# When VectorE takes up an attention pair's sums: a reordering in a fused attention and gated MLP kernel

## The chip, the core and the metric

The kernel runs on one core of a Trainium2 chip. The metric is the device time of one execution in microseconds (us). The core has five engines that matter here, each with its own queue of instructions, worked off in order: TensorE (PE in the profile, its weight loads PEld), VectorE (DVE), ScalarE (ACT), GpSimd (POOL) and SyncE (SP), which starts nearly all DMAs. [...]

## What is computed

The first block is a linear attention without a softmax, for 8 batches, 8 heads, 576 positions and a head width of 64:

```
kv  = einsum('bhsd,bhse->bhde', k, v)          # k^T v, one 64x64 matrix a head
out = einsum('bhsd,bhde->bhse', q, kv)
rms = sqrt(mean(out * out, axis=-1) + 1e-06)   # the mean over a head's 64 values
x   = out / rms * g_norm
```

The heads of a position are then laid side by side, so that x is 4608 tokens of 512 values. The second block is a gated MLP with 2048 hidden values:

```
h = x @ w_in
g = h * erf(softplus(h))
y = g @ w_out
```

q, k, v and g_norm are 32 bit floats. The weights arrive as 64 bit floats, and the kernel turns them into 32 bit ones on the chip.

## The kernel before

**Groups and units.** The tokens are worked in groups of 512. Groups are numbered by `T`; the first group is T = 0. A group's MLP runs over 16 hidden chunks of 128 values, called units (`f`, or `n` counted on through the groups: unit 21 is chunk 5 of group 1). The loop over `n` writes the instructions of group 0 (n = 0 to 15) and group 1 (n = 16 to 31); a second loop, over batches of four units, writes all later groups. While a group's MLP runs, the attention of the next group is done beside it, in four pairs of heads (`p` = 0 to 3). So the second group's pairs (T = 1) lie beside the units 0 to 15, and the third group's (T = 2) beside the units 16 to 31.

**One unit of group 0** on TensorE is a product with w_in into `h_ps` (L1219, 8 matmuls in the profile) and, five units late (`LAG`), a product with w_out into the four `o_ps` (L856, 8 matmuls). ScalarE copies `h_ps` out (L1232) and applies softplus (L1248); each fourth unit it applies erf for four units (L1172). VectorE multiplies h by the result (`gates`, L1100).

**The conversion of the weights** runs beside group 0, item by item in the order `w_order`: one item is one or two chunks of w_in or w_out. Each item has a load (`load_w`, L244 and L249, into one of four `w_raw` buffers), a split on ScalarE (`w_split`, L271, into one of two `w_m` buffers) and a join on VectorE (`w_join`: L281, L284, L287 and L292, four instructions; the last one writes the finished chunk, `w_in_sb` or `w_out_sb`). `weights()` does the split of the next item, the join of the current one and the load of a later one. It is called at a unit's start if the next item falls `due`, and again, in a `while`, before the unit's matmuls.

**One attention pair** is made of pieces that `attention(T, p)` returns and `pieces_of` hangs on units. Each unit has four places: `steps[f][3]` runs at the unit's start, just after the first call of `weights()`; `steps[f][0]` follows it, still ahead of the `while`; `steps[f][1]` runs after the unit's softplus; `steps[f][2]` runs at its end.

- `visit` (the piece `apply`): TensorE computes the results of the pair and k^T v of the *next* pair into one PSUM tile, `at_ps` (L474, L479, L484). ScalarE squares the result o into the tile `qT` (L492), copies o out (L502), copies the two 64-partition halves of k^T v into `kv_other`, each crossed over to the other half of the partitions (L368), and copies the last 64 positions into `x_last` (L507).
- `keep` and `sums` (the piece `after`): VectorE adds the crossed halves to k^T v in `at_ps` and writes `bd_kv` (L372), which the next pair's `visit` needs. It then transposes the squares (L527) and sums them by block (L415, `ms`); for every second pair a few short copies bring the sums together (L428, L429).
- `root` (the roots, on ScalarE), `norm` (on VectorE, with the transposition of the next pair's q, L347) and `split` follow in later units.

`visit` of T = 1, p = 0 is hung on unit 5 (`steps[5][3]`), and its `keep` and `sums` follow at the same place. All other pairs have `visit` at `steps[f+1][1]` and `keep` and `sums` at `steps[f+1][2]`, the end of the same unit.

**The last pair of the third group** (T = 2, p = 3, `both` in the code) is special: its `visit`, in unit n = 29, computes k^T v for *two* next pairs, so that ScalarE makes four crossed copies. Right after it the last units of group 1 (n = 28 to 31) and the *held* units are worked off: four gated units 24 to 27, whose products with w_out are kept back until the MLP of group 1 ends. ScalarE and VectorE cut each of them into three forms, `g_held` (`hold_upper`, L735, on ScalarE; `hold_lower`, L738 and L741, on VectorE), and TensorE multiplies them last (L1116, `held_sums`). A unit of group 1 has two PSUM tiles, `n_ps` and `m_ps` (L800); ScalarE copies n_ps out (L1234) and VectorE adds m_ps (L775) before the next unit may write them. When the held sums are done and the last gates of group 1 are through (L1100), the memory that they held is freed, SyncE loads the first parts of w_out for the loop over batches (L1046), and that loop starts.

The functions that the diff touches:

Of the kernel before, what the change touches and what calls it, by code (L numbers as in the profile page):

```python
# [70 lines left out]
def kernel(  # L71
# [10 lines left out]
    nc = tc.nc  # L82
    P = 128
# [4 lines left out]
    R = S - G  # L88
# [144 lines left out]
    x_last = const.tile([P, KC, G], FP32, name="x_last")  # L233
# [100 lines left out]
    def halves_of(t):  # L334
        return t.rearrange("p (a t) -> p a t", a=2)

    def kv_of(T, p):
        return bd_kv[:, (T * NP + p) % 2, :]
# [10 lines left out]
    def kv_products(T, p, diagonal, beside, first=0):  # L349


        ks, vs = (x.pop((T, p)) for x in (k_sb, v_sb))
        for c in range(CH):
            for i, rows in enumerate(rows_of):
                half = (i + c + first) % 2
                yield half == i, partial(
                    nc.tensor.matmul,
                    (diagonal if half == i else beside)[rows_of[half]],
                    lhsT=ks[rows, c],
                    rhs=vs[rows, c],  # L360
                    start=(c < 2),
                    stop=(c >= CH - 2),
                )

    def kv_beside(at, other, copy, cols=kv_cols):

        for i in range(2):
            copy(other[rows_of[i]], at[rows_of[1 - i], ::-1, cols])  # L368
# [22 lines left out]
    def other_tile(n):  # L391
        t = attp.tile([P, 2, 2, D], FP32, name="kv_other", tag="kv_other")
        return t[:, 0:n]

    def at_tile():
        return at_pool(1).tile([P, 2, G], FP32, name="at_ps", tag="at")
# [14 lines left out]
    def small_tile(name):  # L411
        return attp.tile([P, 2 * BLOCKS], FP32, name=name, tag=name)
# [41 lines left out]
    def attention(T, p):  # L454

        st = {}

        alone = p > 1
        then = divmod(T * NP + p + 1, NP)
        both = (T, p) == (FIRST, NP - 1)  # L460
        more_cols = slice(kv_cols.stop, kv_cols.stop + D)

        two = halves_of

        bd = kv_of(T, p)

        def visit():


            qT = ready.pop((T, p))  # L470
            at = st["at"] = at_tile()
            x = halves_of(qT[:, 0:G])
            for s in rows_of:
                nc.tensor.matmul(  # L474
                    at[s, 1, 2 * P : 2 * P + R], lhsT=bd[s, D : 2 * D], rhs=qT[s, G:S], start=True, stop=True
                )
            st["o"] = at[:, :, 0 : 2 * P]
            for _, product_ in kv_products(*then, at[:, 1, kv_cols], at[:, 0, kv_cols], first=1):
                product_()  # L479
            if both:  # L480
                for _, product_ in kv_products(then[0], 1, at[:, 1, more_cols], at[:, 0, more_cols]):
                    product_()
            for a, i in ((0, 0), (0, 1), (1, 0), (1, 1)):
                nc.tensor.matmul(  # L484
                    at[rows_of[i if a else 1 - i], a, 0 : 2 * P],
                    lhsT=bd[rows_of[i], a * D : (a + 1) * D],
                    rhs=x[rows_of[i], a],
                    start=True,
                    stop=True,
                )  # L490
            st["sq"] = qT[:, 0:G]
            nc.scalar.activation(two(st["sq"]), st["o"], AF.Square, scale=0.125)  # L492
            if T < FIRST:
                if T not in xT:
                    xT[T] = wide.tile([P, KC, G], FP32, name="xT", tag="ab"[T])
                x = xT[T][:, p, :]
            elif p % 2:
                x = x_new.tile([P, G], FP32, name="x", tag="x")
            else:
                x = attp.tile([P, G], FP32, name="x_even", tag="sq_lo")  # L500
            st["x"] = x
            nc.scalar.copy(two(x), st["o"])  # L502
            others = st["others"] = other_tile(2)
            kv_beside(at, others[:, 0], nc.scalar.copy)
            if both:
                kv_beside(at, others[:, 1], nc.scalar.copy, more_cols)
            nc.scalar.copy(x_last[:, p, T * R : T * R + R], at[:, 1, 2 * P : 2 * P + R])  # L507

        def keep():
            others = st.pop("others")  # L510
            kv_sum(*then, st["at"], others[:, 0])
            if both:
                kv_sum(then[0], 1, st["at"], others[:, 1], more_cols)

        def sums():


            if not alone:
                if p == 0:
                    shared["ms"] = small_tile("ms")  # L520
                total = shared["ms"]
            else:
                total = small_tile("ms")
            st["ms"] = total
            side = p if not alone else 0
            t = attp.tile([P, G], FP32, name="sq_t", tag="rms_r")
            nc.vector.transpose(out=t, in_=st["sq"])  # L527
            sum_blocks(total, side, t)
            shared[side] = st
            if not alone and p == 0:  # L530
                return
            n = side + 1
            other = small_tile("ms_other")
            meet(total, other, nc.vector.tensor_copy, n)
            st["n"] = n

        def root(table=True):
            if "n" not in st:
                return
            total, n = st["ms"], st["n"]  # L540
            st["r"], st["u"] = small_tile("rms"), small_tile("rms_u")
            exp_ln_table()
            roots(total, st["r"], st["u"], n)
            if table:
                softplus_table()

        def norm():
            if "n" not in st:
                return
            n = st["n"]  # L550
            refine(st["ms"], st["r"], st["u"], n)
            for i in range(n):
                other = shared[i]
                rb, x = other.pop("sq"), other["x"]
                spread_over(rb, st["u"], i)
                nc.vector.scalar_tensor_tensor(
                    out=x, in0=x, scalar=gm_col, in1=rb, op0=ALU.mult, op1=ALU.mult
                )

        def split():  # L560
            if T < FIRST or "n" not in st:
                return
            for q_ in range(p + 1 - st["n"], p + 1):
                upper(shared[q_ % 2 if not alone else 0]["x"], x_forms[T][0][:, q_])
            for q_ in range(p + 1 - st["n"], p + 1):
                lower(shared[q_ % 2 if not alone else 0].pop("x"), *(form[:, q_] for form in x_forms[T]))

        def loads():
            i = T * NP + p + 2
            if i == (FIRST + 1) * NP + 1:  # L570
                load_q(i)
                load_kv(i + 1)
                load_kv(i + 2)
                return
            load_pair(i, later=True)
            if i == (FIRST + 1) * NP:
                load_kv(i + 1)

        first_ = (partial(prepare, T, p),) if (T, p) == (1, 0) else ()
        then_ = partial(turn, *then)  # L580
        pieces = (first_, (visit, loads), (keep, sums))
        return (*(partial(chain, *group) for group in pieces), root, partial(chain, norm, then_), split)


    twice = {}
# [464 lines left out]
    def pieces_of(T):  # L1050


        steps = [([], [], [], []) for _ in range(FC)]
        for p in range(NP):
            products, apply, after, mean, norm, split = attention(T, p)
            f = (BATCH - 1) * (p + 1) if T < FIRST else BATCH * p

            first = T < FIRST and p == 0
            steps[f][1].append(products)
            steps[f + 2 if first else f + 1][3 if first else 1].append(apply)  # L1060
            steps[f + 2 if first else f + 1][3 if first else 2].append(after)
            with_erf = (f + 2) % BATCH == BATCH - 1
            if T == FIRST and p == NP - 1:
                ending.extend((partial(mean, table=False), norm, split))
                continue
            steps[f + 2][1].append(partial(mean, table=not with_erf))
            steps[f + 3][0].append(norm)
            steps[min(f + 4, FC - 1)][0].append(split)
        return steps
# [5 lines left out]
    others = [("out", f) for f in (*range(FC - BATCH, FC), *range(FC - BATCH))]  # L1075
# [98 lines left out]
    for n in range(FIRST * FC + 1):  # L1174
        T, f = divmod(n, FC)
        if T < FIRST:
            if f == 0:
                steps = pieces_of(T + 1)
# [162 lines left out]
    for m in range(first_batch, batches + 1):  # L1341
        T, b = divmod(m, NB)
# [127 lines left out]
```

## Time and profile before

| what | value |
|---|---|
| median of 3 runs | 890.06 us (888.09 to 891.25) |
| the profiled execution's own time | 889.88 us |
| its span in the profile | 888.1 us |
| busy: PE, DVE, ACT | 874.7 us (98%), 750.4 us (84%), 551.8 us (62%) |
| the loop over batches (256 to 880 us), PE busy | 624.00 of 624.00 us |

The span is the time from the first to the last instruction that the profiler saw. Times in the profile are read from the span's start. In a timeline row the first number is the start, the second the time from the start of the first to the end of the last instruction of the row, then engine, line, operation, the tile written and the tiles read, shapes and the count; in brackets stands the engine's idle time before it and what ended it. Busy times of several engines overlap; what counts is which engine's idle time or work stands on the path that ends last.

### The profile page before, as it was taken

What the parts mean: (1) busy time and instruction counts of PE and PEld (TensorE: products, weight loads), DVE (VectorE), ACT (ScalarE), POOL (GpSimd) and SP (SyncE); (2) the same over time, 40 slices, a digit from 0 to 9 for tenths busy, and PEclk for the clock granted to TensorE, in tenths of its full rate; (3) what the DMA queues carried; (4) which work ended last, traced back from release to release, by engine and by line L of the source; (5) the groups of instructions that cost most, each with busy time, mean ns of one, the idle gap of its engine ahead of it and who ended that gap; (6) DMA issues with size and microseconds to landing.
All of it is one profiled execution on the core that took longest, in us unless ns stands there. A gap on an engine that the chain in (4) does not pass through costs nothing.

```text
span 888.1 us, 13265 instructions
## 1 busy us (share of the span) xinstructions
PE 874.7 (98%) x4842; PEld 653.7 (74%) x4842; DVE 750.4 (84%) x1117; ACT 551.8 (62%) x813; POOL 4.7 (1%) x14
## 2 busy tenths in 40 slices
PE   8989999999999999999999999999999999999998
PEld 4434446656778888888888888888888888888887
DVE  5868997799889898989898989898979797966667
ACT  5947776777665656656574747474756575755552
POOL 2000000000000000000000000000000000000000
PEclk9999999999999999999999999999999999999999
DMA  9964627889799997999699978998797778778861
GB/s 290 296 226 146 198 75 268 305 303 357 252 339 386 342 370 239 381 350 361 209 369 359 349 265 312 375 329 305 272 351 278 290 288 347 291 284 321 323 256 48
DMA packets 136928, 259.88 MB, mean 293 GB/s; under 512 B 78816, under 2 KB 87264, under 8 KB 136864
## 3 DMA queue, kind: packets, MB, share of 16 engines
q1 hardware_dynamic: 136128, 258.09, 81.7%
q10 hardware_dynamic: 544, 0.82, 0.3%
q8 instruction: 38, 0.62, 0.3%
q14 instruction: 26, 0.21, 0.1%
q0 software_dynamic: 192, 0.13, 0.0%
HBM read 224.40 MB, written 34.60 MB: 292 GB/s over the span
## 4 chain that ended last, share of the span: by engine, by line
PE 81%; DVE 8%; ACT 5%; DMA 3%; issue 2%; SPq 1%; DVEq 0%; ACTq 0%
PE n_ps L800 48%; PE m_ps L800 24%; PE h_ps L1219 2%; PE o_ps L856 2%; DVE w_e L287 1%; DMA w_out_parts<-w_out 1%; PE diag_ps L623 1%; PE at_ps L628 1%; DVE w_e L284 1%; ACT s_sb L1172 1%; DVE w_e L281 1%; DVE h_sb L1100 1%; ACT L117 1%; PE warm_ps L1004 1%; DMA w_raw<-in_moe_w_out_dram 1%
## 5 line engine op out<-in xcount | busy, mean ns | idle before, releaser
L800 PE MATMUL n_ps<-w_out_parts,g_forms 128*128 128x512 f32 (+1 forms) x936 | 230.3, 388 | 1.1 <-DMA w_out_parts<-w_out 1.1
L800 PE MATMUL n_ps<-x_forms,w_in_parts 128*128 128x512 f32 x896 | 222.7, 391 | 0.0
L800 PEld LDWEIGHTS n_ps<-w_out_parts,g_forms 128*128 128x128 f32 x936 | 175.1, 188 | 37.5 <-DMA w_out_parts<-w_out 1.8
L800 PEld LDWEIGHTS n_ps<-x_forms,w_in_parts 128*128 128x128 f32 x896 | 167.5, 188 | 38.1 <-issue 3.8
L775 DVE TENSOR_TENSOR h<-m_ps,h 128x512 f32<-128x512 f32 x116 | 78.5, 686 | 65.2 <-PE m_ps L800 65.1
L1381 ACT ACTIVATE s<-h 128x512 f32<-128x512 f32 x112 | 69.3, 632 | 88.3 <-DVE h L775 88.3
L800 PE MATMUL m_ps<-w_out_parts,g_forms 128*128 128x512 f32 x464 | 124.0, 390 | 0.0
L1376 ACT ACTIVATE h<-n_ps 128x512 f32<-128x512 f32 x112 | 66.7, 596 | 85.6 <-PE n_ps L800 83.6
L800 PE MATMUL m_ps<-x_forms,w_in_parts 128*128 128x512 f32 x448 | 119.8, 390 | 0.0
L800 PEld LDWEIGHTS m_ps<-w_out_parts,g_forms 128*128 128x128 f32 x464 | 87.1, 188 | 18.1
L800 PEld LDWEIGHTS m_ps<-x_forms,w_in_parts 128*128 128x128 f32 x448 | 84.1, 188 | 17.4
L775 DVE TENSOR_TENSOR e<-m_ps,e 128x512 f32<-128x512 f32 x116 | 80.1, 692 | 14.2 <-PE m_ps L800 3.7
L856 PE MATMUL o_ps<-w_out_sb,h_sb 128*128 128x512 f32 x192 | 87.1, 596 | 0.1
L735 ACT ACTIVATE g_forms<-h 128x1024 fp32r<-128x1024 f32 x58 | 60.8, 1060 | 39.8 <-PE m_ps L800 21.6
L741 DVE SCALAR_TENSOR_TENSOR g_forms<-g_forms 128x1024 fp32r<-128x1024 f32 x58 | 71.1, 1225 | 2.0
L738 DVE TENSOR_TENSOR g_forms<-h,g_forms 128x1024 fp32r<-128x1024 f32 x58 | 70.6, 1217 | 0.5 <-ACT g_forms L735 0.4
L856 PEld LDWEIGHTS o_ps<-w_out_sb,h_sb 128*128 128x128 f32 x192 | 35.9, 190 | 42.4 <-issue 37.9
L1430 DVE TENSOR_TENSOR h<-h,s 128x1024 f32<-128x1024 f32 x56 | 65.9, 1218 | 0.0
L1219 PE MATMUL h_ps<-xT,w_in_sb 128*128 128x512 f32 x128 | 59.5, 611 | 3.9 <-DVE w_in_sb L292 3.9
L770 DVE SCALAR_TENSOR_TENSOR e<-n_ps,e 128x512 f32<-128x512 f32 (+1 forms) x89 | 59.8, 672 | 4.2 <-PE n_ps L800 4.2
L117 ACT ACT_TABLE_LOAD x41 | 52.6, 1283 | 0.7
L1219 PEld LDWEIGHTS h_ps<-xT,w_in_sb 128*128 128x128 f32 x128 | 24.5, 195 | 36.1 <-issue 33.2
(159 smaller groups left out, 944.3 us busy)
## 6 DMA issues: line engine op xcount, KB each, us to landing
w_out_parts<-w_out SPq DMA_DIRECT2D x116, 768.0 KB, 7.3
w_in_parts<-w_in SPq DMA_DIRECT2D x112, 768.0 KB, 7.0
w_in<-w_new SPq DMA_DIRECT2D x16, 768.0 KB, 4.8
k_sb<-in_k_dram SPq DMA_DIRECT2D x32, 288.0 KB, 5.9
v_sb<-in_v_dram SPq DMA_DIRECT2D x31, 288.0 KB, 5.6
w_raw<-in_moe_w_in_dram SPq DMA_DIRECT2D x16, 512.0 KB, 5.6
w_raw<-in_moe_w_out_dram SPq DMA_DIRECT2D x8, 1024.0 KB, 4.9
out_dram<-e SPq DMA_DIRECT2D x32, 256.0 KB, 4.0
```

Source lines behind the costliest of these rows:

```text
L117: nc.scalar.preload_act_table_set("softplus")
L735: nc.scalar.activation(high, x, AF.Copy, scale=1.0 + 2.0**-13)
L738: nc.vector.tensor_tensor(out=low, in0=x, in1=high.bitcast(FP32), op=ALU.subtract)
L741: nc.vector.scalar_tensor_tensor(out=both, in0=low.bitcast(FP32), scalar=SHIFT, in1=high.bitcast(FP32), op0=ALU.mult, op1=ALU.add,)
L770: nc.vector.scalar_tensor_tensor(out=out_, in0=ps, scalar=scale, in1=out_, op0=ALU.mult, op1=ALU.add)
L775: nc.vector.tensor_tensor(out=out_, in0=ps, in1=out_, op=ALU.add)
L800: nc.tensor.matmul(ps[:, cols], lhsT=weights(form, k), rhs=moving(form, k)[:, cols], start=(form == forms[0] and k == 0), stop=(form == fo ...
L856: nc.tensor.matmul(o_ps[j], lhsT=g[:, j * P : j * P + P], rhs=one(w_out_sb, f), start=(f == 0), stop=last,)
L1219: nc.tensor.matmul(plain[i], lhsT=blocks_of(one(w_in_sb, i % FC))[:, c], rhs=xT[T][:, c, :], start=(c == 0), stop=(c == KC - 1),)
L1376: nc.scalar.activation(h[:, i], n_ps, AF.Copy, scale=SHIFT - 1.0)
L1381: nc.scalar.activation(s[:, i], h[:, i], AF.Softplus)
L1430: nc.vector.tensor_tensor(out=part(h, half), in0=part(h, half), in1=part(s, half), op=ALU.mult)
```

## The change

The pieces `keep` and `sums` of each pair move from the end of a unit (or, for T = 1, p = 0, from the same place as `visit`) to the start of the following unit, `steps[f+2][3]` (for T = 1, p = 0: `steps[f+3][3]`, unit 6), that is, behind the first call of `weights()` of that unit. For the last pair of the third group, the four crossed copies of k^T v and the copy into `x_last` go from ScalarE to VectorE, just ahead of the additions in `keep`, and ScalarE's copy of o goes to `steps[f+2][1]`, a unit later.

The instructions themselves are otherwise the same. In the order of the instructions on each engine only this differs between the two programs:

- VectorE, T = 1, p = 0: three instructions (L372, L527, L415) move behind one w_in item's join, one gate and one w_out item's join. Before, they stood between the gate ahead of that and the first of the joins.
- VectorE, T = 2, p = 3: five copies are added ahead of the two additions (L372).
- ScalarE, T = 2, p = 3: these five copies are gone, and the copy of o (L502) stands behind the first two `g_held`, one copy of n_ps and one softplus.
- TensorE, GpSimd and SyncE: nothing. For the six other pairs nothing moves on any engine: between their old place and their new one no other instruction stands.

```diff
@@ attention(T, p): visit
             st["sq"] = qT[:, 0:G]
             nc.scalar.activation(two(st["sq"]), st["o"], AF.Square, scale=0.125)
+            if not both:
+                copy_out()
+                beside(nc.scalar.copy)
+
+        def copy_out():
             if T < FIRST:
...
             st["x"] = x
             nc.scalar.copy(two(x), st["o"])
+
+        def beside(copy):
             others = st["others"] = other_tile(2)
-            kv_beside(at, others[:, 0], nc.scalar.copy)
+            at = st["at"]
+            kv_beside(at, others[:, 0], copy)
             if both:
-                kv_beside(at, others[:, 1], nc.scalar.copy, more_cols)
-            nc.scalar.copy(x_last[:, p, T * R : T * R + R], at[:, 1, 2 * P : 2 * P + R])
+                kv_beside(at, others[:, 1], copy, more_cols)
+            copy(x_last[:, p, T * R : T * R + R], at[:, 1, 2 * P : 2 * P + R])
 
         def keep():
+            if both:
+                beside(nc.vector.tensor_copy)
             others = st.pop("others")
             kv_sum(*then, st["at"], others[:, 0])
...
         pieces = (first_, (visit, loads), (keep, sums))
-        return (*(partial(chain, *group) for group in pieces), root, partial(chain, norm, then_), split)
+        later = copy_out if both else chain
+        return (*(partial(chain, *group) for group in pieces), later, root, partial(chain, norm, then_), split)
@@ pieces_of(T)
-            products, apply, after, mean, norm, split = attention(T, p)
+            products, apply, after, later, mean, norm, split = attention(T, p)
...
             steps[f][1].append(products)
             steps[f + 2 if first else f + 1][3 if first else 1].append(apply)
-            steps[f + 2 if first else f + 1][3 if first else 2].append(after)
+            steps[f + 3 if first else f + 2][3].append(after)
+            steps[f + 2][1].append(later)
```

## The prediction, made before the changed kernel ran

> **What bounds the kernel now.** I first asked the windows of busy time by stage, then the waits, then the timeline around the two places that the change touches. From 256 us to 880 us TensorE has no gap, so nothing can be won there, and whatever is won before moves that whole block forward. Three rows of the windows (columns: stretch, its length, PE busy, PEld, DVE, ACT, POOL, granted clock, DMA share, GB/s):
>
> ```profile
> 53.00:58.00 5.00, 5.00 (x9) 2.06 (x8) 4.79 (x7) 0.70 (x1) 0.00 (x0) 0.66 1.01 342
> ...
> 223.00:228.00 5.00, 5.00 (x15) 3.97 (x16) 4.82 (x13) 2.15 (x4) 0.00 (x0) 0.66 1.05 385
> ...
> 256.00:880.00 624.00, 624.00 (x3454) 513.00 (x3453) 534.31 (x755) 374.33 (x522) 0.00 (x0) 1.00 0.86 312
> ```
>
> The granted clock is 0.66 in the first two: a third of the cycles is missing, which is half clock for 3.4 of 5 us. Both stretches follow a TensorE gap, and the change touches both. The first, in the waits from 20 to 135 us:
>
> ```profile
> DVE bd_kv L372 <- ACT x_last L507: 8.2, 2, 5.1
> ...
> PE h_ps L1219 <- DVE w_in_sb L292: 3.9, 2, 3.2
> ```
>
> and in the timeline:
>
> ```profile
> 43.25 0.69 DVE L1100 TENSOR_TENSOR h_sb<-h_sb,s_sb 128x512 f32<-128x512 f32 x1
> ...
> 46.78 0.21 ACT L507 COPY x_last<-at_ps 128x64 f32<-128x64 f32 x1
> ...
> 47.03 0.29 DVE L372 TENSOR_TENSOR bd_kv<-at_ps,kv_other 128x128 f32<-128x128 f32 x1 [3.10 <-ACT x_last L507]
> ...
> 48.58 0.68 DVE L281 TENSOR_SCALAR w_e<-w_raw 128x1024 f32<-128x1024 f32 x1
> ...
> 52.65 5.37 PE L1219 MATMUL h_ps<-xT,w_in_sb 128*128 128x512 f32 x8 [3.18 <-DVE w_in_sb L292]
> ...
> 68.02 0.29 DVE L372 TENSOR_TENSOR bd_kv<-at_ps,kv_other 128x128 f32<-128x128 f32 x1 [5.13 <-ACT x_last L507]
> ```
>
> VectorE stands 3.10 us before pair 0's sums because ScalarE copies late; the w_in join queued behind them (48.58) comes late for it, and TensorE stands 3.18 us for that join. Its next 8 matmuls take 5.37 us where others of L1219 take 3.60. The second place, around 221 us:
>
> ```profile
> 220.07 1.08 ACT L368 COPY kv_other<-at_ps 64x128 f32<-64x128 f32 x4
> ...
> 221.40 0.49 DVE L372 TENSOR_TENSOR bd_kv<-at_ps,kv_other 128x128 f32<-128x128 f32 x2 [1.77 <-ACT x_last L507]
> ...
> 222.31 0.59 ACT L1234 ACTIVATE h<-n_ps 128x512 f32<-128x512 f32 x1
> ...
> 222.95 0.50 PE L800 MATMUL n_ps<-x_high,w_new 128*128 128x512 f32 x1 [1.79 <-ACT h L1234]
> ```
>
> **Part A, the sums of pair 0 behind two joins.** Removed from the path: VectorE's wait. The gate at 43.25 ends at 43.94; the join, 3.92 us long in the trace (48.58 to 52.50), can start at 43.97 and end at 47.89. Its w_raw was loaded by an issue at 28.70, and the split of it is ScalarE's L271 at 42.97 to 44.13, ahead of everything that is late. (Were it the next L271, 46.89 to 48.04, the join would end at 49.3.) TensorE's w_out products start at 45.88, and 8 of them take 3.43 us to the start of what follows (57.86 to 61.29), so TensorE asks for the chunk at 49.31 and finds it. Gain: 52.65 - 49.31 = 3.34 us. With no gap I expect no clock loss: 57.86 - 52.65 = 5.21 becomes 3.43, another 1.78. Sum 5.12 us; bounds 3.3 (the slow clock stays) and 5.3.
>
> Does it reach the end? The moved block's reader is pair 1's visit on TensorE, then at 64.82 - 5.12 = 59.70. VectorE's order is now join to 47.89, gate 0.60, join 3.95, block 1.55 (47.03 to 48.58), so the block ends at 53.99 and the transposed q, queued behind it, at about 54.8. That cover is some 5 us; without it TensorE would stand for the excess. VectorE then does what took 5.91 us before (56.98 to 62.89) and is at pair 1's sums at 59.9, while ScalarE's x_last is ready at 67.98 - 5.12 = 62.87. So it waits there 3.0 instead of 5.13 us, and its two waits shrink from 8.2 to 3.0, that is, by the same 5.1. From here TensorE, VectorE and ScalarE have their old distances, 5.12 us earlier, and up to 121 us neither TensorE nor VectorE waits again. SyncE's order is unchanged: its load behind the first join waits for L287, and goes 4.7 us earlier (51.31 to 46.6). The k and v that pair 1's visit needs follow it; 52.33 to 64.82 is 12.5 us for a transfer that lands after 4.4 to 6.1, so 0.4 us less costs nothing.
>
> **Part B, the last pair of the third group.** ScalarE loses the copy of o (0.59 from start to start), four copies (1.09) and x_last (0.10 to 0.21): the two g_held and the copy of n_ps behind them come 1.78 us earlier, at 220.6 for the latter. It then waits only for TensorE's n_ps, which began at 218.06; TensorE can go on at 221.2. The copy of o now stands between a softplus and two g_held, 0.5 us on ScalarE, which I cost at nothing: the softplus ahead of it waits for VectorE and comes earlier by about that.
>
> VectorE gains work: four 64x128 copies from PSUM. Nearest row: L387 copies of 64x128, 246.82 to 247.85 for four, 0.26 each, and 0.25 for x_last (L644, twice the size, took 0.28): 1.3 us, bounds 1.2 and 1.5. They start at 219.62, when the second gate ends, without waiting for ScalarE's copies. So the additions start at 220.9 instead of 221.40: VectorE is 0.5 us earlier, not 1.8. Queued behind it are the add that frees m_ps (224.09, then 223.6 to 224.2) and the four g_held lowers. TensorE, 1.7 us earlier at 221.2, has done its n_ps at 223.1 and now stands for m_ps until 224.2, then for g_held: the second unit's are ready at 228.03 - 0.48 = 227.55. From there TensorE has 0.92 us of products to go to where it stood at 229.24, so it is there at 228.47, 0.77 us earlier, and the chain behind it (e at 234.43, the last gate at 241.2, the load of w_out issued at 241.86) is paced by that. B is 0.8 us.
>
> Bounds of B: 1.8 above (the additions cost VectorE nothing). Below zero too: the slow clock of 223 to 228 may come back, because TensorE still stands about 1.1, 1.0 and 0.4 us in small pieces. Half clock for 3.4 us on the held products, where VectorE no longer hides it, costs 1.7: B = -0.9. [...]
>
> **Sum.** 5.1 + 0.8 = 5.9 us from the profiled execution's own 889.88 gives 884.0; that execution stands 0.18 below the median 890.06, so on the median's scale 884.2. With the slow clock in B it is 885.9. I forecast 884.4. This kernel's runs spread from 888.09 to 891.25, so about 0.3% (2.7 us) is what a measurement can tell: faster means below 887.4, slower above 892.7.
>
> **Rivals.**
> - *Only the wait goes, not the clock* (chance 0.12): TensorE's slow stretch at 53 us comes anyway, or another late input at 49.3 takes half of the gap. Against it: each low clock in these rows follows a gap. A is 3.3 or less, B near zero or below: 886.6 to 888.
> - *Swallowed by transfers* (0.09): DMA is at 0.90 share from 171 to 222 us and PE waits 1.06 us for w_out_parts at 254.75. If these loads are paced by the memory and not by their issue, the loop starts when it did: 889 to 890. Against it: SyncE's longest waits are for compute, and the w_out load waited 8.7 us for the gate L1100 at 241, so it moves along.
> - *Slower* (0.07): the new small gaps keep TensorE at half clock from 223 us on. Each us at half clock costs 0.5; to undo 5.9 and lose another 2.7 it takes 17 us of it, about all of TensorE's work up to 240. The price would be 893. Against it: both slow stretches in the trace end after 3.4 us, though TensorE was dense in them.
> - *The change does little of what it says*: the sums of seven pairs are moved in the code, but the order of instructions changes for pair 0 of the second group alone. So A rests on one place; it is the place with the gap.
>
> **How the numbers follow.** Forecast 0.72 (883 to 886.5, both clock cases of B), rivals 0.12, 0.09 and 0.07; the fourth is no time of its own. Low end: A 5.3 and B 1.8 give 883.0, and 0.8 for the spread of a median: 882.2. High end: the first rival, 888.0. Faster: 0.72 and two thirds of the first rival, 0.80; same 0.13; slower 0.07.
>
> **What the profile after would show.** Right: no wait of TensorE for w_in_sb near 49 us, clock 1.00 from 43 to 68, VectorE's first wait for x_last gone and the second about 3.0 us; at the last pair TensorE's wait for the n_ps copy gone, a new one of about 1 us for VectorE's add of m_ps; the loop over batches 4 to 6 us earlier and as long as before. Wrong: a new TensorE wait for bd_kv or q at 59.7, clock under 1.00 past 228 us, or a wait for w_out_parts longer by what was won.

## The result, and the profile after

The changed kernel takes 884.03 us (median of 16 runs, 882.87 to 889.0), beside 888.95 us for the kernel before in the same set (median of 16, 887.21 to 891.25). The ratio is 0.9952, with a 95% interval of 0.9939 to 0.9965. The profiled execution took 885.19 us, its span 883.4 us. The change adds lines, so that places have new numbers: L800 is now L813, L775 is L788, L1219 is L1233, L1116 is L1130, L1100 is L1114, L507 is L517, L738 and L741 are L751 and L754, L1046 is L1059. L368 and L372 stay.

The windows of busy time, in the stretches shown before (columns as there: stretch, length, PE, PEld, DVE, ACT, POOL, granted clock, DMA share, GB/s); the loop over batches now begins earlier, so its row ends at 875:

```profile
43.00:53.00 10.00, 10.00 (x24) 4.37 (x23) 9.59 (x13) 7.42 (x13) 0.00 (x0) 1.00 0.82 271
53.00:58.00 5.00, 5.00 (x13) 2.28 (x12) 4.90 (x7) 2.27 (x3) 0.00 (x0) 1.00 0.88 250
223.00:228.00 5.00, 5.00 (x19) 4.05 (x18) 4.68 (x9) 3.94 (x6) 0.00 (x0) 0.78 0.95 244
256.00:875.00 619.00, 619.00 (x3433) 508.83 (x3432) 530.29 (x749) 370.48 (x518) 0.00 (x0) 1.00 0.86 312
```

From 43 to 53 us TensorE has no gap any more, and from 53 to 58 us the granted clock is 1.00 (0.66 before). At the second place, from 223 to 228 us, it is 0.78. The waits from 20 to 135 us:

```profile
DVE bd_kv L372 <- ACT x_last L517: 3.1, 1, 3.1
...
PE h_ps L1233 <- DVE w_in_sb L292: 0.7, 1, 0.7
```

VectorE's 8.2 us in two waits have become one of 3.1; TensorE's 3.9 us have become 0.7, and that one is the other wait, at 23 us. In the timeline of the first place:

```profile
43.51 0.68 DVE L1114 TENSOR_TENSOR h_sb<-h_sb,s_sb 128x512 f32<-128x512 f32 x1
...
44.12 0.69 DVE L281 TENSOR_SCALAR w_e<-w_raw 128x1024 f32<-128x1024 f32 x1
...
46.93 1.23 DVE L292 CUSTOM_DVE_ANT_0 w_in_sb<-w_e,w_m 128x2048 uint16<-128x2048 uint16 x1
...
52.63 0.28 DVE L372 TENSOR_TENSOR bd_kv<-at_ps,kv_other 128x128 f32<-128x128 f32 x1
...
63.18 0.29 DVE L372 TENSOR_TENSOR bd_kv<-at_ps,kv_other 128x128 f32<-128x128 f32 x1 [3.12 <-ACT x_last L517]
```

The join (44.12) starts directly behind the gate; it stood at 48.58 before. Pair 0's sums come at 52.63 without a wait, pair 1's at 63.18 instead of 68.02. The second place, first VectorE, then TensorE:

```profile
214.84 1.21 DVE L368 COPY kv_other<-at_ps 64x128 f32<-64x128 f32 x4
216.09 0.23 DVE L517 COPY x_last<-at_ps 128x64 f32<-128x64 f32 x1
216.23 0.48 DVE L372 TENSOR_TENSOR bd_kv<-at_ps,kv_other 128x128 f32<-128x128 f32 x2
...
218.91 0.68 DVE L788 TENSOR_TENSOR h<-m_ps,h 128x512 f32<-128x512 f32 x1
```

```profile
219.65 1.20 PE L813 MATMUL m_ps<-x_both,w_new 128*128 128x512 f32 x4 [1.19 <-DVE h L788]
221.58 3.62 PE L1130 MATMUL o_ps<-w_place,g_held 128*128 128x512 f32 x8 [0.72 <-DVE g_held L754]
```

TensorE's wait of 1.79 us for ScalarE's copy of n_ps is gone, and in its place stand 1.19 us for VectorE's add and 0.72 us for a g_held. The eight held matmuls behind it take 3.62 us; the granted clock is 0.50 from 221.79 to 225.21 us, that is, during nearly all of them.

**Where the time went.** Four marks serve here: the first sums, pair 1's sums, the first e and the issue of the w_out load. The rows of pair 1's sums are shown above; the others are, before the change:

```profile
38.34 0.29 DVE L372 TENSOR_TENSOR bd_kv<-at_ps,kv_other 128x128 f32<-128x128 f32 x1
...
234.43 0.60 ACT L1147 ACTIVATE e<-n_ps 128x512 f32<-128x512 f32 x1 [1.72 <-PE n_ps L1116]
...
241.86 2.65 SPq L1046 DMA_DIRECT2D w_out_parts<-w_out  x4
```

and after it:

```profile
38.62 0.29 DVE L372 TENSOR_TENSOR bd_kv<-at_ps,kv_other 128x128 f32<-128x128 f32 x1
...
230.28 0.60 ACT L1161 ACTIVATE e<-n_ps 128x512 f32<-128x512 f32 x1 [2.76 <-PE n_ps L1130]
...
237.71 3.19 SPq L1059 DMA_DIRECT2D w_out_parts<-w_out  x4
```

In all executions the first sums (L372) stand near 38.5 us, ahead of everything that the change touches. Measured from there, pair 1's sums were at 68.02 - 38.34 = 29.68 us before and are at 63.18 - 38.62 = 24.56 us after: 5.12 us earlier. From there to the first e (L1147, now L1161) the kernel before took 234.43 - 68.02 = 166.41 us, the changed one 230.28 - 63.18 = 167.10: 0.69 us are given back. From e to the load of w_out it is 7.43 us in both. Together with 0.28 us of a later start, 0.28 us less from that load's issue to the product that needs it, and 0.27 us less from there to the end, this makes the whole difference: 0.28 - 5.12 + 0.69 - 0.28 - 0.27 = -4.7 us, from 889.88 to 885.19.

### The profile page after: what moved, and what is told of

The parts are those of the page before. It is cut to its first block, busy times and chain, and to the rows that moved or that the text cites. A ratio compares the mean times of both kernels' runs of the same rounds, so it can differ in the third digit from the quotient of the medians.

```text
span 883.4 us, 13264 instructions
## 1 busy us (share of the span) xinstructions
PE 873.4 (99%) x4842; PEld 653.1 (74%) x4842; DVE 751.2 (85%) x1122; ACT 550.7 (62%) x808; POOL 4.7 (1%) x14
## 4 chain that ended last, share of the span: by engine, by line
PE 81%; DVE 9%; ACT 4%; DMA 3%; issue 2%; SPq 0%; DVEq 0%; ACTq 0%
PE n_ps L813 47%; PE m_ps L813 24%; PE h_ps L1233 3%; PE o_ps L869 2%; DVE w_e L287 1%; DMA w_out_parts<-w_out 1%; PE diag_ps L636 1%; PE at_ps L641 1%; DVE h_sb L1114 1%; DVE w_e L284 1%; DVE w_new L775 1%; PE o_ps L1130 1%; PE warm_ps L1017 1%; DVE w_e L281 1%; DMA w_raw<-in_moe_w_out_dram 1%
## 5 line engine op out<-in xcount | busy, mean ns | idle before, releaser
L813 PE MATMUL n_ps<-w_out_parts,g_forms 128*128 128x512 f32 (+1 forms) x936 | 229.9, 388 | 0.8 <-DMA w_out_parts<-w_out 0.8
L813 PE MATMUL n_ps<-x_forms,w_in_parts 128*128 128x512 f32 x896 | 222.6, 390 | 0.0
L813 PEld LDWEIGHTS n_ps<-w_out_parts,g_forms 128*128 128x128 f32 x936 | 175.1, 188 | 37.1 <-DMA w_out_parts<-w_out 1.2
L813 PEld LDWEIGHTS n_ps<-x_forms,w_in_parts 128*128 128x128 f32 x896 | 167.4, 188 | 38.3 <-issue 3.9
L788 DVE TENSOR_TENSOR h<-m_ps,h 128x512 f32<-128x512 f32 x116 | 78.5, 686 | 65.6 <-PE m_ps L813 65.5
L813 PE MATMUL m_ps<-w_out_parts,g_forms 128*128 128x512 f32 x464 | 123.9, 389 | 0.0
L813 PE MATMUL m_ps<-x_forms,w_in_parts 128*128 128x512 f32 x448 | 119.7, 389 | 0.0
L813 PEld LDWEIGHTS m_ps<-w_out_parts,g_forms 128*128 128x128 f32 x464 | 87.1, 188 | 18.1
L813 PEld LDWEIGHTS m_ps<-x_forms,w_in_parts 128*128 128x128 f32 x448 | 84.1, 188 | 17.5
L788 DVE TENSOR_TENSOR e<-m_ps,e 128x512 f32<-128x512 f32 x116 | 80.2, 692 | 14.0 <-PE m_ps L813 3.7
L754 DVE SCALAR_TENSOR_TENSOR g_forms<-g_forms 128x1024 fp32r<-128x1024 f32 x58 | 71.1, 1225 | 2.0
L751 DVE TENSOR_TENSOR g_forms<-h,g_forms 128x1024 fp32r<-128x1024 f32 x58 | 70.5, 1216 | 0.5 <-ACT g_forms L748 0.4
L1233 PE MATMUL h_ps<-xT,w_in_sb 128*128 128x512 f32 x128 | 57.8, 595 | 0.7 <-DVE w_in_sb L292 0.7
L1418 ACT ACTIVATE s<-s 128x1024 f32<-128x1024 f32 x50 | 50.6, 1054 | 0.3
```

What stands on the lines that cost most here:

```text
L751: nc.vector.tensor_tensor(out=low, in0=x, in1=high.bitcast(FP32), op=ALU.subtract)
L754: nc.vector.scalar_tensor_tensor(out=both, in0=low.bitcast(FP32), scalar=SHIFT, in1=high.bitcast(FP32), op0=ALU.mult, op1=ALU.add,)
L788: nc.vector.tensor_tensor(out=out_, in0=ps, in1=out_, op=ALU.add)
L813: nc.tensor.matmul(ps[:, cols], lhsT=weights(form, k), rhs=moving(form, k)[:, cols], start=(form == forms[0] and k == 0), stop=(form == fo ...
L1233: nc.tensor.matmul(plain[i], lhsT=blocks_of(one(w_in_sb, i % FC))[:, c], rhs=xT[T][:, c, :], start=(c == 0), stop=(c == KC - 1),)
```

## The experiments

The theory was the prediction's: the sums of pair 0 win 5.1 us, of which 1.78 by the clock, and the last pair of the third group little. Rivals: the clock comes back anyway; the w_out load swallows part; VectorE's leftover wait of 3 us costs too. The runs were made in two sets with the kernel before beside them (888.40 us, 26 runs; 888.27 us, 12 runs), and four single executions, each with its profile (before_look1 to 3 and after_look). Their marks in one table, all read from the timelines: the clock in the two stretches, the time from the first sums to pair 1's sums, to the issue of the w_out load, and what TensorE waits for that load.

| run | clock at 53 to 58 | clock at 222 to 228 | to pair 1 | to the load | wait | profiled time |
|---|---|---|---|---|---|---|
| before | 0.66 | 0.72 | 29.68 | 203.52 | 1.06 | 889.88 |
| before_look1 | 0.66 | 0.72 | 29.67 | 203.46 | none | 888.70 |
| before_look2 | 0.66 | 1.00 | 29.68 | 203.34 | 2.58 | 890.77 |
| before_look3 | 1.00 | 1.00 | 27.98 | 201.64 | none | 887.35 |
| fill | 1.00 | 0.72 | 27.99 | 201.77 | 1.17 | 888.61 |
| b_only | 1.00 | 0.77 | 27.97 | 202.54 | 1.13 | 889.03 |
| after | 1.00 | 0.73 | 24.56 | 199.09 | 0.77 | 885.19 |
| after_again | 1.00 | 1.00 | 24.57 | 197.97 | 1.12 | 884.07 |
| after_look | 1.00 | 1.00 | 24.56 | 197.89 | 2.57 | 886.91 |
| a_only | 1.00 | 1.00 | 24.55 | 198.24 | 1.78 | 885.26 |
| a_pair1 | 1.00 | 1.00 (0.72 at 216 to 222) | moved | 197.53 | 1.64 | 884.17 |
| pair1_too | 1.00 | 0.81 (0.91 at 216 to 222) | moved | 198.17 | none | 883.19 |
| sums_later | 1.00 | 1.00 | 24.56 | 197.26 | none | 882.63 |
| best | 1.00 | 1.00 | moved | 196.30 | 1.43 | 883.01 |

**One part alone: pair 0's sums.** On the kernel before:

```diff
-            steps[f + 2 if first else f + 1][3 if first else 2].append(after)
+            steps[f + 3 if first else f + 1][3 if first else 2].append(after)
```

> Part A alone: the sums of pair 0 behind the two joins, the last pair of the third group as before. Theory (the gap of TensorE at 49 us and the slow clock behind it are the whole of A): 5.1 us less than the kernel before, ratio 0.994, that is at least as fast as the whole change. Rival (part B carries a share of the measured 4.3 to 4.9 us): 4.1 us less or fewer, ratio 0.9955 or above.

Measured: 885.26 us (9 runs), ratio 0.9955 (0.9940 to 0.9971). Pair 1's sums come at 24.55 us, just where the whole change has them; the timeline has VectorE's row there and TensorE's at the start of the loop:

```profile
63.10 0.29 DVE L372 TENSOR_TENSOR bd_kv<-at_ps,kv_other 128x128 f32<-128x128 f32 x1 [3.09 <-ACT x_last L507]
```

```profile
250.41 0.73 PE L800 MATMUL n_ps<-w_out_parts,g_forms 128*128 128x512 f32 x2 [1.78 <-DMA w_out_parts<-w_out]
```

The ratio lies on the border that the expectation drew for its rival, so the time alone does not decide between them; pair 1's sums at the place of the whole change, and the next run, do. Within the interval this part is all of the change's gain (0.9952 for the whole), though this profiled execution lost 0.7 us more to the load of w_out than that of before.

**The other part alone: the last pair.** On the changed kernel, pair 0's sums back to their old place:

```diff
-            steps[f + 3 if first else f + 2][3].append(after)
+            steps[f + 2][3].append(after)
```

> Part B alone: VectorE makes the crossed copies of the last pair of the third group, ScalarE copies o a unit later, the sums of pair 0 stay where they were. Theory: 0.8 us less where TensorE keeps its clock, 0.6 us more where the clock falls to half behind the new small gaps; ratio 0.999 to 1.001. Rival (ScalarE's 1.8 us reach the end): ratio 0.998.

Measured: 889.50 us (12 runs), ratio 1.0007 (0.9996 to 1.0019): worth nothing. One thing in its profile was not expected. The wait of TensorE for the join is back, 3.2 us at its longest (the waits of this run, 20 to 135 us), and yet the clock behind it is whole, 1.00 from 53 to 58 us (its windows):

```profile
PE h_ps L1233 <- DVE w_in_sb L292: 3.9, 2, 3.2
```

```profile
53.00:58.00 5.00, 5.00 (x12) 2.31 (x13) 4.79 (x7) 2.33 (x4) 0.00 (x0) 1.00 1.00 327
```

**The gap filled.** On the kernel before, a product whose result is overwritten, ahead of unit 6's product with w_in; it makes 8 matmuls in the profile, 3.43 us from start to start of the next:

```diff
+            if n == 6:
+                for c in range(KC):
+                    nc.tensor.matmul(
+                        plain[n],
+                        lhsT=blocks_of(one(w_in_sb, n - 1))[:, c],
+                        rhs=xT[T][:, c, :],
+                        start=True,
+                        stop=True,
+                    )
```

> The kernel before with four more matmuls (3.4 us) in TensorE's gap ahead of unit 6, whose sums are thrown away; nothing else is moved, so the w_in chunk comes as late as before. Theory (the gap makes the clock fall): no slow matmuls behind it, 1.7 us less than before, ratio 0.998, and the wait itself stays. Rival (the clock falls there by itself): no difference, ratio 1.000.

Measured: 888.78 us (12 runs), ratio 0.9994 (0.9979 to 1.0009). TensorE stands there no more, the clock stays at 1.00 from 53 to 58 us, and the join comes as late as ever. Pair 1's sums, with VectorE's wait ahead of them, are 1.7 us earlier than in the first profile of before (27.99 against 29.68 us from the first sums):

```profile
66.93 0.29 DVE L372 TENSOR_TENSOR bd_kv<-at_ps,kv_other 128x128 f32<-128x128 f32 x1 [3.45 <-ACT x_last L507]
```

So the clock term is there in the profile, but the median does not move. The interval runs from 1.9 us less to 0.8 us more, so it still holds the expected 1.7 us; together with b_only's whole clock it raised the next question.

**How often does the low clock come?** Three more executions of the kernel before, unchanged, each with its profile.

> The kernel before once more, for its profile alone: how often does the low clock come behind the 3.2 us gap of TensorE at 49 us? Theory (it comes in most executions, as the mean clock of the executions suggests): 53 to 58 us at 0.66 in at least two of the three looks, TensorE's 8 matmuls behind the gap at 5.4 us. Rival (it comes seldom, and the term of 1.78 us of the sum counts for little): 1.00 in at least two of the three and 3.6 us for these matmuls. Time 888 to 890 us either way.

> As the look before it: the second of three looks at the kernel before. Theory 0.66 from 53 to 58 us, rival 1.00.

> As the look before it: the third of three looks at the kernel before. Theory 0.66 from 53 to 58 us, rival 1.00.

Measured: 0.66, 0.66 and 1.00, two of three as the theory said. All have the same wait of 3.2 us. Here are the rows of the third one's timeline, TensorE's and VectorE's:

```profile
53.24 3.67 PE L1219 MATMUL h_ps<-xT,w_in_sb 128*128 128x512 f32 x8 [3.18 <-DVE w_in_sb L292]
```

```profile
66.91 0.29 DVE L372 TENSOR_TENSOR bd_kv<-at_ps,kv_other 128x128 f32<-128x128 f32 x1 [3.44 <-ACT x_last L507]
```

The same 8 matmuls took 5.37 us in the first profile, and VectorE's wait at pair 1 was 5.13 us. Of the five profiles with this gap (four of before, and b_only) three show the low clock. The mean clock of every execution points the same way. One stretch of 3.4 us at half clock is 1.7 of 888 us, or 0.002 of the mean, and in the 14 profiles a mean of 0.999 or more goes with no such stretch. Of the 50 executions of before and b_only in the two sets 5 have a mean clock of 0.999 or more; of the 68 of the kernels whose gap is closed or filled (the 16 of the result among them) 45 have, and of fill alone, which changes nothing else, 7 of 12. But the mean does not tell the first place from the second.

**What the low clock goes with.** The traces hold the moments at which the granted clock changes. In before these are 53.27, 56.68, 223.94 and 227.35 us, in after 221.79 and 225.21. In both the clock from each fall to the rise behind it is 0.50, for 3.413 us, and the two falls of before are 50 times 3.413 us apart. So the idle time is counted here in steps of 3.413 us, which in each execution are laid at that execution's own changes of the clock; a gap that a border of two steps cuts counts in two parts. TensorE's idle time by step, summed from its rows, with the clock that stands in the next step (half is 0.50, whole 1.00):

| place | execution | idle us in a step | clock in the next step |
|---|---|---|---|
| gap at 49 us | before, before_look1, before_look2 | 2.80, 2.64, 2.43 | half |
| gap at 49 us | before_look3 (cut in two), b_only (cut in two) | 1.68 + 1.50, 1.41 + 1.77 | whole |
| around 220 us, old order | before, before_look1, fill, a_pair1 | 1.80, 1.93, 1.94, 1.90 | half |
| around 220 us, old order | before_look2, before_look3, a_only | 1.74, 1.71, 1.63 | whole |
| around 220 us, new order | after, b_only, pair1_too | 1.91, 1.91, 1.71 | half |
| around 220 us, new order | after_again, after_look | 1.27, 1.19 | whole |

From 30 to 876 us there are 11 falls in the 14 profiles: ten of them behind 1.80 us or more in one step, pair1_too's behind 1.71, and no step without a fall has more than 1.77. Behind the same gap of 3.2 us the half clock stands in the three profiles in which 2.43 to 2.80 us of it lie in one step, and does not in the two in which no step holds more than 1.77 us of it. By what the clock is set these profiles do not show.

**The changed kernel again**, in the second set and once more for its profile:

> The changed kernel once more, on the chip that the other three of this call run on, so that they can be set beside it. Both theories: 0.995 of before (0.994 to 0.9965).

> The changed kernel's third profile. Two showed from pair 0 of the third group to the first e 93.96 us with the clock at 0.73 and 92.82 with it at 1.00 from 222 to 228 us; the kernel before took 93.28 at 0.72. Theory (in the new order the low clock is no longer hidden by VectorE): 93.9 if the clock is below 0.8, 92.8 if it is 1.00. Rival (the two profiles differ for another reason): the other way round, or 93.3 whatever the clock.

Measured: 884.07 us (7 runs), ratio 0.9958 (0.9941 to 0.9974); the single execution after_look took 886.91 us. Both had a clock of 1.00 from 222 to 228 us, and from pair 0 of the third group to the first e they took 92.82 and 92.76 us, against 93.96 in the first profile with low clock (and 94.03 in b_only, which has the same order there and low clock too). The kernel before took 93.28 and 93.22 with low clock, 93.09 and 93.11 without. So low clock costs the new order 1.2 us here and the old one 0.15. The reason is in the timelines: in the old order TensorE waits for a g_held in the undisturbed execution, and a slow clock ahead of it only uses up that wait. In before_look3:

```profile
225.59 2.52 PE L1116 MATMUL o_ps<-w_place,g_held 128*128 128x512 f32 x8 [0.73 <-DVE g_held L741]
```

In the profile of before, with low clock, the same product has no such wait. In the new order the stall comes first and the half clock falls on the held products behind the wait, where nothing hides it: 3.62 us for these 8 matmuls in the first profile of after, 2.53 in after_again, at whole clock:

```profile
221.22 2.53 PE L1130 MATMUL o_ps<-w_place,g_held 128*128 128x512 f32 x8 [0.74 <-DVE g_held L754]
```

The profile of after_look also shows what spreads these times: TensorE waited 2.57 us for w_out_parts at 250 us, all in one step, and the clock fell behind it (0.83 from 250 to 260 us), a third place for the same thing. In before_look2 a wait of 2.58 us there lay in two steps, with 1.50 and 1.08, and the clock from 250 to 260 us is 1.00. The rows of after_look:

```profile
250.45 0.92 PE L813 MATMUL n_ps<-w_out_parts,g_forms 128*128 128x512 f32 x2 [2.57 <-DMA w_out_parts<-w_out]
```

```profile
250.00:260.00 10.00, 9.55 (x35) 7.77 (x36) 5.91 (x11) 7.18 (x9) 0.00 (x0) 0.83 1.02 317
```

**VectorE's other wait.** On the changed kernel, pair 1's sums of the second group moved behind the next join and gate as well:

```diff
-            steps[f + 3 if first else f + 2][3].append(after)
+            steps[f + 3 if first else f + 2][1 if (T, p) == (1, 1) else 3].append(after)
```

> The changed kernel with pair 1's sums of the second group moved behind the next w_out join and gate as well, so that VectorE's last wait of 3.1 us for x_last at 60 us is gone. Theory (TensorE is dense from 43 to 134 us, so this wait costs nothing): same time as the changed kernel, ratio to the kernel before 0.995. Rival (VectorE's conversion paces this stretch): up to 3 us less again, ratio 0.992.

Measured: 883.30 us (6 runs), ratio 0.9935 (0.9920 to 0.9949). This lies between the theory's 0.995 and the rival's 0.992, and its interval overlaps that of the changed kernel; the theory that the wait costs nothing is not borne out by the profile either, as the next run shows. VectorE's wait is 1.09 us instead of 3.12, now at the gate ahead of the sums:

```profile
65.10 0.69 DVE L1114 TENSOR_TENSOR h_sb<-h_sb,s_sb 128x512 f32<-128x512 f32 x1 [1.09 <-ACT s_sb L1186]
65.71 0.28 DVE L372 TENSOR_TENSOR bd_kv<-at_ps,kv_other 128x128 f32<-128x128 f32 x1
```

The same place for `after` was then tried on the kernel before, so that the last pair of the third group stays as it was:

```diff
-            steps[f + 2 if first else f + 1][3 if first else 2].append(after)
+            steps[f + 3 if first else f + 2][1 if (T, p) == (1, 1) else 3].append(after)
```

> Of the change only the move of pair 0's sums, and with it the sums of pair 1 of the second group moved in the same way; the last pair of the third group is as before, copies on ScalarE. Theory (VectorE's leftover wait of 3 us at pair 1 costs 1 to 1.7 us, and part B is worth nothing by itself): 0.993 to 0.994 of before, as the changed kernel with pair 1 moved (0.9935). Rival (what that run won, it won by part B, which needs the earlier VectorE to pay): 0.9955, as the move of pair 0 alone.

Measured: 882.45 us (6 runs), ratio 0.9939 (0.9921 to 0.9956), the theory's value, with the rival's 0.9955 at the edge of the interval. By the load's issue this move is worth 198.24 - 197.53 = 0.71 us here and 199.09 - 198.17 = 0.92 us on the changed kernel. It is not the 3 us of the wait, since TensorE is dense there. How it gets through is seen at the end of the conversion, on ScalarE and TensorE of the changed kernel:

```profile
116.15 1.15 ACT L772 ACTIVATE w_new<-w_in_sb 128x512 fp32r<-128x512 f32 x2 [2.50 <-DVE w_out_sb L292]
...
125.85 0.80 PE L813 MATMUL n_ps<-x_high,w_new 128*128 128x512 f32 x1
```

and of the one with pair 1 moved:

```profile
114.47 1.15 ACT L772 ACTIVATE w_new<-w_in_sb 128x512 fp32r<-128x512 f32 x2 [0.96 <-DVE w_out_sb L292]
...
125.39 0.80 PE L813 MATMUL n_ps<-x_high,w_new 128*128 128x512 f32 x1
```

VectorE's conversion ends 1.7 us earlier, ScalarE's wait for it falls from 2.50 to 0.96 us, and the start of group 1, which needs ScalarE's cut, comes 0.46 us earlier. The rest of the 0.92 us comes in the first units of group 1: TensorE's product that begins at 137.98 us in the changed kernel begins at 137.08 here. What makes it there was not tried out.

**The additions behind the add.** On the changed kernel, in the last pair only, the squares' sums are split off from the additions and put behind the next unit's add:

```diff
-        pieces = (first_, (visit, loads), (keep, sums))
-        later = copy_out if both else chain
+        pieces = (first_, (visit, loads), (keep,) if both else (keep, sums))
+        later = (copy_out, sums) if both else (chain, chain)
...
-            steps[f + 2][1].append(later)
+            steps[f + 2][1].append(later[0])
+            steps[min(f + 3, FC - 1)][1].append(later[1])
```

The edit came out smaller than the expectation's first sentence says: the copies and the additions stay ahead of the add that frees m_ps; only the transposition and the sums of squares behind them (L539 to L429) moved, 2.3 us on VectorE.

> The changed kernel, but in the last pair of the third group VectorE's copies of k^T v and its sums stand behind the add that frees m_ps of the last unit instead of ahead of it. Theory (part B gives nothing because these copies and additions hold up that add, for which TensorE then stands 1.19 us, and 0.72 us for a g_held): both waits go or shrink below 0.3 us each, the first e comes 1 to 2 us earlier after the sums of pair 1 of the second group than the 167.1 us of the changed kernel, and the time is 1 to 2 us under the changed kernel's: 0.993 of before. Rival (TensorE would stand just as long for ScalarE's copy of n_ps and its halves of g_held, or the load of w_out sets the loop's start): the first e comes again at 166.4 to 167.1 us, or the loop's wait for w_out_parts grows by what was won, and the time is the changed kernel's, 0.995.

Measured: 883.38 us (6 runs), ratio 0.9940 (0.9925 to 0.9955). TensorE's wait for m_ps is gone; the wait for a g_held is longer instead (1.22 us, against 0.74 in after_again), so only one of the two waits went:

```profile
224.74 1.21 PE L1131 MATMUL o_ps<-w_place,g_held 128*128 128x512 f32 x4 [1.22 <-DVE g_held L754]
```

To the load it is 0.71 us less than in after_again (197.97 to 197.26), less than the expected 1 to 2 us. From pair 1's sums to the first e it takes 165.27 us; the 167.1 us that the expectation set beside it were an execution with low clock, and after_again, with whole clock as here, has 165.97. The six executions have mean clocks of 0.999 or 1.0, but the changed kernel had many of these too.

**Both together**, the edit of sums_later and that of pair1_too:

> The kernel before this in the list, and with the sums of pair 1 of the second group a place earlier on VectorE as well (ahead of a wait of 3 us, as in the run before this call that measured 0.9935). Theory that both waits cost: the two gains add up, 0.991 to 0.992 of before, 1.5 us under each of the two alone, and the loop over batches is the bound from then on. Rival (the load of w_out sets when the loop starts): no faster than the better of the two alone, 0.993, with a wait for w_out_parts of over 1.5 us.

Measured: 882.17 us (6 runs), ratio 0.9929 (0.9914 to 0.9943), the fastest of all. To the load it is 196.30 us, 0.96 less than sums_later and 1.67 less than after_again: the two gains add up there. The ratio lies between the theory's and the rival's. By the medians it is 1.9 us faster than after_again; the intervals of best, sums_later, pair1_too and a_pair1 overlap, so their order among each other stays open.

## Why the prediction was right, and where its sum was not

**The place and the path of A: right.** The join starts at 44.12 us (43.97 predicted; this execution runs 0.28 us late), pair 0's block ends at 54.25 us (53.99), and x_last is ready for pair 1 at 63.14 us (62.87). VectorE's wait there is 3.12 us (3.0). From pair 1's sums to pair 0 of the third group it is 73.13 us before and 73.14 after, so nothing is lost on the way.

**The size of A: one of its two terms is not in every execution.** The gap's term was put at 3.34 us. Between executions that both have whole clock it measured 27.98 - 24.56 = 3.42. The clock's term was put at 1.78 and measured 29.68 - 27.98 = 1.70, in the three of five profiles that have it: from these A is the 5.12 us of the prediction, from the other two it is 3.42. The step that failed is "With no gap I expect no clock loss", with the whole 1.78 us charged to it, and its ground "each low clock in these rows follows a gap": each low clock of the 14 profiles does, but it was read the other way round, as if each such gap brought the low clock. One profile could not show that. The lower bound of 3.3 covered it. Weighted by the five profiles, A is 3.42 + 0.6 * 1.70 = 4.4 us. The table by steps gives another estimate. No step without a fall has more than 1.77 us; if that holds for other executions, a gap of 3.18 us goes without low clock only where a border cuts it into two parts of 1.77 us at most. This leaves 0.36 of 3.41 us, about one execution in ten if the borders lie at random, and A would be 3.42 + 0.9 * 1.70 = 5.0 us. The times do not decide between the two: a_only alone measured 888.40 - 885.26 = 3.1 us less, with an interval from 2.6 to 5.3.

**B: nothing in the mean, because its sign goes with the clock.** The steps of TensorE's and VectorE's new waits held: the additions 0.33 us earlier beyond A (0.5 predicted), 1.19 us of waiting for m_ps (1.1), 0.72 us for a g_held. The copies and x_last took 1.39 us (1.3) from start to the additions; the four copies alone took 1.21 us, against 1.08 on ScalarE before. What came out was not +0.8 but, from pair 1's sums to e, 166.31 us in the mean of four profiles before and 166.32 in the mean of three after. With whole clock B is +0.3 us (166.23 against 165.94), with low clock -0.7 (166.39 against 167.10). The second is the mechanism that was named for the lower bound of -0.9: "Half clock for 3.4 us on the held products, where VectorE no longer hides it, costs 1.7". It comes in three of the five profiles of this order (after, b_only, pair1_too). The 0.8 us were too much also in the good case: the wait for a g_held that TensorE has in the old order was not seen, since the low clock of that one profile had swallowed it. So in both orders VectorE paces this point, and its 0.3 us are all that is won: the product behind that wait starts 225.59 - 66.91 = 158.68 us after pair 1's sums in before_look3 and 221.22 - 62.83 = 158.39 in after_again.

**The sum, and why the time still fits.** 5.9 us were predicted; A of 4.4 to 5.0 and B of 0 give 4.4 to 5.0, and 888.95 - 884.03 = 4.9 and 888.27 - 884.07 = 4.2 were measured. That the time came so close (884.4 predicted, 884.03 measured) is in part luck: the median of three runs that it started from, 890.06 us, lay 1.1 us above the later median of sixteen, and the gain that was taken off was too large by 1.0 us. The profile that was taken of before was also one with both low clocks.

**The rivals.** *Only the wait goes* expected the low clock at 53 us to come back. It did not in any of the nine profiles without the gap (1.00 from 53 to 58 us in all of them); it is right only in this, that the clock's term cannot always be won: it was missing from part of the executions before. *Swallowed by transfers*: TensorE waits between 0 and 2.58 us for w_out_parts in four profiles of before and between 0.77 and 2.57 in three of after. The load moved along with the rest; these waits spread the times and do not take the gain, though a few tenths of a us in either direction cannot be excluded with so few profiles. *Slower*: each low clock ended after about 3.4 us here too (3.413 us in before and after). That *the change does little of what it says* held: one pair's move carries it all.

## What to carry to other kernels

A work item that waits for another engine should not stand ahead of one that is ready and that somebody waits for: moving three instructions behind two joins brought 3.4 us without an instruction less. Before a low clock is put into a sum, look at several profiles of the same kernel, because one shows what can come and not how often: here the same gap of 3.2 us was followed by 3.4 us at half clock in three of five profiles. When a stall is moved to another engine, see what stands behind it: a slow clock ahead of a wait cost 0.15 us here, and the same slow clock behind the wait 1.2 us.

## What was not expected of the hardware

- The same gap of 3.2 us was followed by 3.4 us at half clock in three profiles and by whole clock in two, with the same instructions around it; in the three 2.43 to 2.80 us of it lay in one step of 3.41 us, in the two it lay in two steps, with 1.68 and 1.50 us (before_look3) and 1.41 and 1.77 (b_only).
- The clock fell behind steps with little more than half of their 3.41 us idle: behind 1.80 us in before and 1.71 in pair1_too. Behind 1.71 us in before_look3 and 1.77 in b_only it did not. The ends of matmuls are modelled in these profiles, so the last few hundredths of a us are not sure.
- Behind two short waits of 1.19 and 0.72 us, both in one step (after), the clock fell to 0.50. Of 1.11 and 0.74 us in after_again 1.27 us lay in one step, and the clock from 222 to 228 us is 1.00.
- From its issue to the product that needs it the load of w_out took from 12.6 to 14.4 us where TensorE waited for it, and in two executions of the same kernel before (before_look1 and before_look3) it was there in time; this alone spreads the times by over 2 us.
